# A spectral filter beside a two-layer network: fewer warm-up matmuls, remainder rows copied by ScalarE, and a new written-out order

## The chip, the cores and the metric

The kernel runs on one core of one Trainium2 chip. A core has five engines that work side by side, each with its own queue of instructions: TensorE (PE in the profile; its weight loads are shown as PEld), VectorE (DVE), ScalarE (ACT), GpSimd (POOL) and SyncE (SP), which here issues most DMAs. They share the on-chip memory SBUF (128 partitions); matmuls write to PSUM, eight banks of 512 fp32 values in each partition. The metric is the device time of one execution in microseconds (us), and what is compared is the median of several executions.

## The reference: what is computed

The input `x` has 2048 rows (tokens) of 640 values. It is normalised row by row, `xn = layernorm(x)`, and two branches that read `xn` are added to `x`:

```python
def _A_ref(x, w_r, w_i):                      # spectral filter
    X = rfft2(x, axes=(-2, -1))               # 2048 x 321 complex
    y = irfft2(X * (w_r + 1j * w_i), s=(2048, 640))
def _B_ref(x, w1, b1, w2, b2):                # two-layer network
    h = gelu(x @ w1 + b1)                     # 640 -> 1536
    return h @ w2 + b2                        # 1536 -> 640
return x + _A_ref(xn, ...) + _B_ref(xn, ...)
```

Inputs and output are bf16.

## The kernel before, in words

**Tiles.** The tokens are split into 16 tiles, c = 0 to 15, of 128 tokens each. Token 16p+c lies in partition p of tile c, so a tile is strided over the sequence, and the transform over the sequence splits into a step of length 128 and one of length 16.

**Norm.** For each tile DVE computes statistics (`stats`, L480, two halves; `mv`, L482), then `ve` (L490), POOL a power for `rstd` (L491), and DVE the normalised tile (L510). Norms are written to a buffer of two slots, each for a pair of tiles (`xn{pair}`, a part of the tensor `T`), so a pair's norm waits until all that read the slot's former pair is through.

**Network branch.** Layer 1 needs `xn` transposed (`xnT`). Tiles 0 to 3 are transposed by PE (L528, through `ident`) and copied from PSUM by DVE or ACT (L533 to L537). Tiles 4 to 15 are transposed by DMA, issued on SP (L519). Layer 1 of tiles 0 and 1 is cut into small pieces, so that each piece needs one slice of W1 (`hpsa`, L567 to L595); tiles 2 and 3, 4 to 7, 8 to 11 and 12 to 15 follow as blocks (`hps0` to `hps3`, L596 to L613). ACT applies the gelu and adds `b1col`. That column is made from the loaded row b1 by twelve tiny matmuls (L464, "b1 turned") and one copy on ACT (L466). Layer 2 accumulates twelve pieces per tile in PSUM (`second`, L758). For some tiles (`KEEP`) DVE moves its result to SBUF early (`kept`, L771).

**Spectral branch.** DVE folds each pair of normalised tiles twice (L540, L544), PE transforms along the tokens (`aps`, L550), then along the width (`bps`, table `etab`), then the length-16 step (`cps`). DVE multiplies with the filter `W` (L678, L682), PE goes back (`dps`), and DMA transposes on SP (L703) bring the result to `XV`. The last way back, `eps` (L726, table `getab`), works on six groups of chunks with 2, 3, 3, 3, 3, 2 chunks (`GROUPS`). Its weights are the columns of `XV` for chunk c: 128 values 16 elements apart. The width 160 of each quarter is split into 128 rows and 32 remainder rows; `width` (L615) makes for each chunk four 128-row matmuls and four 32-row ones, the remainders of the four quarters side by side in plane 4 of `XV`. DVE unfolds, a last matmul (L777) adds the result to layer 2 in PSUM, DVE writes the sum to `W1` (L780), and a DMA stores it.

**Start.** PE first multiplies zeros (`idle`, L409), in two ops of 39 and 8 matmuls, both ahead of the first transposes in the order.

**What sets the order.** Each piece of work is an "op" with a list of what it reads and writes. `ORDER` (L253) is a text that names each op once by its number, with the letter of its engine (s SP, p PE, a ACT, d DVE, g POOL) and its PSUM or buffer slots. `arrange` (L145) puts the ops into the five queues in that order, and `sync` (L161) derives the semaphore waits. Priorities, durations, landing times (`at=`), `gate` and `hard` fed the planner that once wrote the text; they have no effect on the program when `ORDER` is given. A queue works strictly in its order, so an op that waits holds all behind it on its engine.

Of the kernel before, what the change touches and what calls it, by code (L numbers as in the profile page):

```python
# [254 lines left out]
53a 289p:2 269p:1 23s 239p:5 259p:3 240p 127d 250p 24s 280p 270p 290p 133d:0 260p 25s 128p:4 130p:7 281p 129d 26s 251p 131a 132d 291p 261p 242p 252p 27s 241p 272p 68d 292p 271p 28s  # L255
243p 282p 69d 283p 253p 29s 262p 65d 244p 273p 274p 30s 284p 66d 254p 255p 70d 263p 67d 293p 245p 71d 134d:1 264p 72g 285p 135d 275p 137d 276p 256p 141d:0 278a 294p 246p 286p 144d
258a 142p:4 136d 248a 145p:7 143d 265p 247a 295p 146d 287a 266p 296p 148d:0 257a 305p:5 77d 288a 311p:7 147d 268a 323p:4 306p 85d 267a 314p:6 307a 312p 89d 315p 277a 332p:5 93d
297a 324p 92d 320p:3 298a 302p:0 101d 313a 321p 325a 100d 333p 326p:7 322a 152d:0 94d 308p:4 90d 316a 327p 151d 138p:1 91d 328a 139p 97d 309p 334a 95d 317p:6 98d 96g 140a 329p:7
102d 99d 330p 103d 149d 299p:5 5g 104g 184d:0 318p 331a 303p 150d 300p 182d 319a 7g 154p:1 81d 304a 153p 183s 197d:1 573p:6 301a 195d 310a 574p 186d:0 155a 196s 590p:4 187d 84d
575p 74d 591p 76d 198s 82d 576p 73d 592p 191d:1 185s 78d 189d 577p 188d 190d 578p 75d 83d 200d:0 31s 593p 79d 199d 32s 80g 192p:1 86d 594p 579d 33s 193p 113d 595p 34s 87d 203d:1  # L260
88g 374p:6 35s 204d 156d:1 375p 596d 157s 386p:0 376a 116d 377p:4 158d 194a 201d 159s 404p:7 114d 171d:0 398p:5 202d 115d 169d 36s 405p 161d:0 206p:1 172s 108d 406a 205p 117d 387p
207a 109d 389p:7 160d 170s 401p:6 118d 164d:1 388a 119d 165d 378p 120g 106d 37s 402p 163d 110d 379a 162d 390p 38s 221d:1 403a 399p 105d 39s 166p:0 223d 400a 167p 107d 356p:4 224s
111d 225d:0 391a 112g 226d 357p 359p:7 227d:1 358a 40s 229d 347p:5 228d 168a 230d 222s 173d:0 348p 174d 360p 210d:0 41s 231p:0 177d:0 361a 335p:6 208d 42s 349a 178d 232p 175d 336p
211s 176d 234a 212d:0 344p:7 213d 337a 180p:3 215d:1 209s 179p 216d 233a 345p 214d 350p:6 217d 181d 346a 43s 218p:0 219p 44s 365p:7 220a 45s 351p 338p:4 46s 352a 446p:0,0 47s 48s
366p 448d 447a 49s 339p 428p:5 50s 51s 443p:0,1 429p 445a 444d 410p:6 340a 733d 411p 367a 461p:0 434p:4 462a:1 463d:0 435p 430a 464p:0 436a 416p:5 235g 465d 466a 417p 412a 236g
471d:0 449p:0,1 418a 472d 237g 425p:7 450a 468d:1 238g 422p:4 467d 451a 426p 423p 469d:0 353p:5 473d:1 424a 470d 485p:0 427a 431p:4 487d:1 486a:0 432p 474d 626p:6 433a 478p:0
380p:4 480d:0 479a:2 381p 475p:0 382a 354p 477d 476a 419p:4 355a 484s 420p 488p:0 413p:5 490a 489d 483s 414p 421a 495d:1 455p:0,0 415a 481s 496d 392p:4 457a 456d 482s 383p:5 492d:0
393p 384p 394a 491d 452p:0,1 385a 498d:0 494d:1 368p:4 453a 454d 369p 341p:5 370a 497d 493d 512p:0 371p:4 513a:1 514d:0 372p 499p:0 373a 342p 500d:2 501a:0 362p:4 343a 363p 509p:0
395p:5 511d 510a 396p 515d:1 502p:0 627p 503a 504d 628p 364a 520d:0 505s 458p:0,1 397a 519d 629p 459a 507s 460d 609p:4 610p 516d 506s 536p:0 521d:0 630p 538a:0 518d:1 611p 517d
508s 537a:1 522d 631p 533p:0 612p 535a 534d 613p 632d 526p:0 614p 543d:0 527a:1 662p:6 540d:1 528a:2 663p 544d 523p:0 664p 615d 524a 665p 546d:1 525a 530s 645p:4 539d 666p 545d  # L270
667p 529s 541d:0 542d 646p 668d 647p 531s 547p:0 698p:6 548d:0 532s 699p 549d:1 700p 648p 550p:0 701p 551a 552d 702p 554s 703p 649p 704d 650p 556s 440p:7 651d 441p 553s 437p:4 442a
407p:5 555s 408p 564p:6 565p 438p 566p 557p:0 567p 558d:1 559a 568p 439a 560d:0 569p 409a 561d 583p:0 562d:0 563d 681p:4 585a:0 584d 570p 682p 571d:7 619p:0 586d:0 572g 587d 683p
620a:1 589d:1 684p 621a 588d 685p 686p 655p:0 687d 622d:0 600p:6 657a:0 743d 601p 623d 656a 602p 636p:4 580p:0 616p:2 581d:6 637p 638p 617d:2 639p 625d:0 618g 603p 624d 640p 658d:0
652p:2 604p 653d:0 641p 654g 605p 606p 642p 607d:3 691p:0 643d:5 608g 672p:6 659d 693a:1 644g 673p 692a 633p:4 674p 660d:0 675p 634d:7 676p 661d 635g 726p:0 695d:0 708p:4 582g
727a:0 694d 677p 728a 709p 678p 597p:0 679d:2 669p:2 710p 598d:0 680g 711p 688p:6 670d:7 712p 599g 697d:1 713p 696d 734p:0 689d:4 717p:2 714p 718p 690g 715d:5 719p 729d:0 671g 735p
730d 753p:7 720p 716g 705p:4 736p 706d:2 737p 732d:0 707g 721p 731d 722p 723p 738p 724d:1 739p 725g 744p:4 745p 746p 740p 747p 741d:7 754p 755p 748p 756p 749p 742s 750p 757p 762p:6
751d:0 758p 759p 763p 764p 760d 752s 765p 766p 767p 761s 768p 769d 770s
"""


# [9 lines left out]
AHEAD = 2  # L290
CHAIN = "b0 b1 c00 c01 b2 c10 c11 d00 d01 b3 b4 c20 c21 d10 d11 b5 c30 c31 d20 d21 d30 d31".split()
XASPLIT = [((0, 1, 2, 3, 4),)] * 7 + [((0, 1), (2, 3, 4))]
WARM = (39, 8)
FILTER = {7: 4}


def bass_parallel_sum__spectral_gfnet__dense_activation_gelu__prompt_kernel(
# [21 lines left out]
    with ExitStack() as es:  # L319
# [113 lines left out]
        for j, at in enumerate((5.92, 6.93, 7.9, 9.75, 10.7)):  # L433
            if j == 3:
                load_x(2, 2, next(pr), at=8.75)
            load(W1[:, F * j:F * j + F], w1v[:, j, :], B_w1s[j], 393216, prio=next(pr), at=at)
        load(gtab[:], const["G"], B_g, 524288, prio=next(pr), at=12.0)
        for c, at in zip(range(4, 16, 2), (13.2, 14.7, 15.5, 16.3, 17.1, 17.9)):
# [13 lines left out]
        for ri, wsrc in enumerate((A_w_r, A_w_i)):  # L452
            for half in range(4):
# [4 lines left out]
                else:  # L458
# [36 lines left out]
        for pair in range(8):  # L495
# [10 lines left out]
            for n in range(2):  # L506
# [15 lines left out]
                for j0, j1, engs in ((0, 2, ["dve"]), (2, 5, ["act"])) if c < 2 else ((0, 5, ["dve", "act"]),):  # L522
                    nj = j1 - j0
                    tps = Buf(f"tps{c}", psum, 1, ZONE["tps"])

                    def xt(e, _, n=n, xnv=xnv, tps=tps, j0=j0, j1=j1):
                        for j in range(j0, j1):
                            ins = e.transpose(psb(tps.slot, [[1, 512]]).bitcast(BF)[:, 128 * j:128 * j + 128], xnv(n, 128 * j, [[1, 128]]), ident[:])  # L528
                        return ins
                    tp = K.op([("pe", nj * mm_us(128))], pr, xt, reads=[B_xn, xn, B_id], writes=[tps], segs=[("128", nj * mm_us(128))])  # L530
# [290 lines left out]
```

## Time and profile before

| | us |
|---|---|
| median of 3 runs | 148.84 |
| lowest, highest | 148.66, 149.22 |
| the profiled execution | 149.58 |
| its span, first to last instruction | 147.8 |

| engine | busy us | share of the span |
|---|---|---|
| PE | 141.9 | 96% |
| PEld (weight loads) | 90.5 | 61% |
| DVE | 110.0 | 74% |
| ACT | 72.3 | 49% |
| POOL | 21.5 | 15% |

A row of the timeline reads: start, duration (of a run of like instructions together), engine, line, operation, output<-input, shape, count, and in brackets how long the engine was idle before it and what ended that. A row of the groups reads: busy time, mean ns of one, idle time before and its releasers. Durations of matmuls include their run through the array, so neighbours overlap: what a matmul costs the stream is the step from its start to the next start. PEclk, the granted clock, is 1.00 throughout, also where matmuls step slowly at the start. Some matmul records are missing from the trace (1677 of 1692).

### The profile page before, as it was taken

How to read it: one execution, taken by the hardware profiler on the slowest of the kernel's cores; microseconds unless marked ns; L12 is line 12 of the kernel's file. 1: busy time of each engine (PE TensorE's matmuls, PEld its weight loads, DVE VectorE, ACT ScalarE, POOL GpSimd, SP SyncE). 2: the span in 40 equal slices, each digit the busy share in tenths (PEclk: the TensorE clock that was granted, in tenths of full speed). 3: DMA queues.
4: the chain of work that ended last, by engine and by line, in shares of the span. 5: the costliest groups of instructions: out<-in, count | busy, mean ns of one | idle time of the engine just before them, and what ended most of it. 6: DMA issues, size and time to landing. Idle time of an engine off the chain costs nothing.

```text
span 147.8 us, 3951 instructions
## 1 busy us (share of the span) xinstructions
PE 141.9 (96%) x1677; PEld 90.5 (61%) x1692; DVE 110.0 (74%) x240; ACT 72.3 (49%) x118; POOL 21.5 (15%) x35
## 2 busy tenths in 40 slices
PE   7999999999799999999999999999999999999993
PEld 7999995655456645445644545555666656655573
DVE  2688999999996367856966979864099787769543
ACT  3615995047598579977775756121075400430000
POOL 1002040301200005000000000000002024545620
DMA  5999999569999998988700670475302107777974
GB/s 119 305 402 399 378 388 132 113 141 135 165 163 160 158 161 218 350 334 45 141 4 0 41 138 10 89 93 106 71 4 24 20 4 84 93 89 91 114 87 114
DMA packets 29843, 21.01 MB, mean 142 GB/s; under 512 B 20225, under 2 KB 27137, under 8 KB 29826
## 3 DMA queue, kind: packets, MB, share of 16 engines
q1 hardware_dynamic: 27232, 15.84, 49.7%
q0 software_dynamic: 2592, 4.92, 17.8%
q8 instruction: 13, 0.21, 0.6%
q14 instruction: 4, 0.03, 0.1%
q10 hardware_dynamic: 2, 0.00, 0.0%
HBM read 13.54 MB, written 5.24 MB: 127 GB/s over the span
## 4 chain that ended last, share of the span: by engine, by line
PE 89%; DVE 5%; DMA 2%; issue 2%; SPq 1%
PE ps L383 88%; DMA xnT<-T 2%; DVE W L780 1%; DVE stats L480 1%; PE ps L528 1%; DVE T L544 1%; DVE T L510 1%; DVE T L540 1%; DVE X L771 1%; SPq L519 1%; DVE mv L482 0%; DVE warm L399 0%; DVE ve L490 0%
## 5 line engine op out<-in xcount | busy, mean ns | idle before, releaser
L383 PE MATMUL ps<-xnT,W 128*128 128x512 bf16 (+2 forms) x336 | 56.9, 320 | 1.0 <-DMA xnT<-T 1.0
L383 PE MATMUL ps<-W,gT 128*128 128x128 bf16 (+3 forms) x382 | 55.0, 292 | 1.5 <-issue 1.0
L383 PEld LDWEIGHTS ps<-W,gT 128*128 128x128 bf16 x396 | 30.1, 98 | 22.5 <-issue 1.7
L383 PEld LDWEIGHTS ps<-xnT,W 128*128 128x128 bf16 x336 | 31.4, 114 | 18.5 <-ACT gT L611 2.8
L611 ACT ACTIVATE gT<-ps,b1col 128x512 bf16<-128x512 f32 (+1 forms) x48 | 28.4, 638 | 15.1 <-PE ps L383 15.1
L787 POOL DMA_DIRECT2D out_dram<-W x14 | 12.3, 990 | 71.0 <-DVE W L780 71.0
L394 ACT ACTIVATE Wf<-ps 128x960 bf16<-128x960 f32 (+1 forms) x10 | 8.5, 888 | 17.9 <-PE ps L383 17.9
L480 DVE BATCH_NORM_STATS2 stats<-X 128x6 f32<-128x320 bf16 x32 | 14.0, 477 | 2.1 <-DMA X<-in_A_x_dram 2.1
L678 DVE TENSOR_TENSOR T<-Y,Wf 128x1288 bf16<-128x1288 bf16 x16 | 12.5, 822 | 0.0
L491 POOL TENSOR_TENSOR rstd<-ve,mhalf 128x2 f32<-128x2 f32 (+1 forms) x8 | 6.0, 744 | 31.9 <-DVE ve L490 31.8
L395 DVE CAST Y<-ps 128x644 bf16<-128x644 f32 x7 | 5.8, 829 | 5.4 <-PE ps L383 5.4
L394 ACT ACTIVATE Xb<-ps 128x960 bf16<-128x960 f32 (+1 forms) x7 | 8.0, 1166 | 3.4 <-PE ps L383 3.3
L544 DVE TENSOR_TENSOR T<-T 128x512 bf16<-128x512 bf16 (+1 forms) x32 | 9.0, 313 | 0.2
L394 ACT ACTIVATE XV<-ps 128x1280 bf16<-128x1280 f32 (+2 forms) x8 | 8.9, 1109 | 0.5 <-PE ps L383 0.5
L395 DVE CAST Xb<-ps 128x960 bf16<-128x960 f32 (+1 forms) x5 | 5.5, 1105 | 4.2 <-PE ps L383 4.2
L394 ACT ACTIVATE Y<-ps 128x644 bf16<-128x644 f32 x9 | 6.3, 708 | 4.1 <-PE ps L383 4.0
L510 DVE TENSOR_SCALAR T<-X,mv,rstd 128x640 bf16<-128x640 bf16 x16 | 6.9, 441 | 1.5 <-POOL rstd L491 1.0
L383 PE MATMUL ps<-getab,XV 32*128 32x160 bf16 (+1 forms) x128 | 7.5, 242 | 0.0
L540 DVE TENSOR_TENSOR T<-T 128x640 bf16<-128x640 bf16 x16 | 7.4, 480 | 0.1
L739 DVE TENSOR_TENSOR Wf<-Wf 128x960 bf16<-128x960 bf16 (+1 forms) x12 | 6.7, 596 | 0.9 <-PE ps L383 0.8
L780 DVE TENSOR_TENSOR W<-ps,b2bc 128x640 bf16<-128x640 f32 x6 | 4.8, 821 | 3.3 <-PE ps L383 3.3
L383 PE MATMUL ps<-etab,XV 32*128 32x160 bf16 (+1 forms) x128 | 7.2, 232 | 0.0
(53 smaller groups left out, 123.1 us busy)
## 6 DMA issues: line engine op xcount, KB each, us to landing
out_dram<-in_A_x_dram POOLq DMA_DIRECT2D x4, 640.0 KB, 7.3
X<-in_A_x_dram SPq DMA_DIRECT2D x7, 320.0 KB, 9.4
out_dram<-W POOLq DMA_DIRECT2D x14, 160.0 KB, 3.4
W<-in_B_w_dram SPq DMA_DIRECT2D x5, 384.0 KB, 5.8
W<-in_B_w_dram SPq DMA_DIRECT2D x3, 640.0 KB, 12.8
Wf<-in_A_w_r_dram SPq DMA_DIRECT2D x7, 160.5 KB, 3.9
Wf<-in_A_w_i_dram SPq DMA_DIRECT2D x7, 160.5 KB, 4.6
gtab<-c_G SPq DMA_DIRECT2D x1, 512.0 KB, 9.1
```

What stands on the lines that cost most here:

```text
L383: ins = e.matmul(o_, lhsT=lw, rhs=rh, start=st, stop=sp_, skip_group_check=True)
L394: return e.activation(dst(), src(), ACT.Copy, scale=scale)
L395: return e.tensor_copy(dst(), src())
L480: st_ops.append(K.op([("dve", 0.393)], pr, lambda e, _, c=c, h=h: e.bn_stats(stats[:, c, 6 * h:6 * h + 6], view(X, c * D + H2 * h, [[1, H2 ...
L510: o = K.op([("dve", 0.356)], pr, lambda e, _, c=c, n=n, xnv=xnv: e.tensor_scalar(out=xnv(n, 0, [[1, D]]), in0=view(X, c * D, [[1, D]]), sc ...
L540: K.op([("dve", 0.39)], pr, lambda e, _, k=k, op=op, xnv=xnv, x1v=x1v: e.tensor_tensor(out=x1v(H2 * k, [[D, 2], [1, H2]]), in0=xnv(0, 0, [ ...
L544: ring_ops.append(K.op([("dve", 0.333 if w == 128 else 0.136)], pr, lambda e, _, op=op, x1v=x1v, xfv=xfv, o_=o_, o0=o0, o1=o1, w=w: e.tens ...
L611: K.op([("act", act_us(128 * nt, 1) + 0.02)], pr + PRIO["gelu"], lambda e, _, c0=c0, nt=nt, fc=fc, hps=hps: e.activation(gT[:, fc, 128 * c ...
L678: filt_ops.append(K.op([("dve", 0.738)], pr, lambda e, _, k=k, Y=Y, TB=TB, pair=pair: e.tensor_tensor(out=view(TT, TB.slot * 8 * KP + k * ...
L739: K.op([("dve", 0.068 + n / 6)], pr + 3, lambda e, _, k=k, op=op, y2=y2, yf=yf, n=n: e.tensor_tensor(out=view(Wf, YF + yf.slot * 3 * D + ( ...
L780: K.op([("dve", dve_us(w))], 95, lambda e, _, os_=os_, fps=fps, o0=o0, w=w, xo=xo, base=base: e.tensor_tensor(out=view(W1, OST + os_.slot ...
L787: last.append(K.op([("pool", 0.9)], 450, lambda e, _, c=c, os_=os_: e.dma_start(ov[:, c, :], view(W1, OST + os_.slot * D, [[1, D]]), accum ...
```

## The change

- The warm-ups are one op of 31 matmuls instead of two of 39 and 8; the matmuls that turn b1 come right behind them, ahead of the first transposes (before: behind these).
- For the last four groups of the way back (gi 2 to 5) ACT first copies the remainder plane's columns of the group to `T`, chunk by chunk side by side, and the 32-row matmuls take their weights from that copy. The 128-row ones and the first two groups stay as they are. PE waits for the copy (`B_xr`).
- `ORDER` is written anew. Among much else: on SP the loads of `etab` and `mtab` move behind the DMA transposes of tiles 8 to 11; all five of the first W loads (before: four) come ahead of the transposes of tiles 4 to 7, whose order is now 5, 6, 7, 4 (before: 4, 5, a W load, 7, 6). On DVE the copy for tile 1 moves ahead of the two foldings of tile 0, tile 2's copy goes to ACT, and the norm of tile 8 loses some work ahead of it. A few PSUM copies swap between ACT and DVE. Behind the filter, more of layer 2 stands between the last DMA transposes and the first group of the way back.
- The changed `at=` values, durations and `hard=` only concern the planner.

```diff
-9s 2a 0d 4g 6g 125p:1 3g 11a 10s 8p:6 12s 13s 14s 15s 55d 54d 16s 1d 17s 56d 60d 57a 18s 58a 59d 121d:1 19s 61d 124p:1 20s 122p:0 52p:7 62d 21s 123d 126a 63d 64g 22s 279p:0 249p:6
...
+9s 2a 0d 7g 8p:1 3g 11a 10s 5g 4g 12s 13s 14s 15s 54d 55d 16s 1d 17s 56d 60d 57a 52p:3 18s 58a 59d 121d:1 19s 61d 122p:0 20s 124p:2 62d 21s 53a 63d 123d 125a 64g 22s 238p:5 288p:4
...
-WARM = (39, 8)
+WARM = 31
...
-        idle(WARM[0], 0.1067 * 32 + (WARM[0] - 32) * mm_us(128))
+        idle(WARM, WARM * mm_us(128))
...
-        pe([("128", 0.7)], 200, lambda: [(psb(B_b1ps.slot, [[1, 1]], fc), part(gT, 0, 1, 512 * (fc // 4) + fc % 4, [[4, 128]]), ident[0:1, 0:1], True, True)
+        b1op = pe([("128", 0.5)], 200, lambda: [(psb(B_b1ps.slot, [[1, 1]], fc), part(gT, 0, 1, 512 * (fc // 4) + fc % 4, [[4, 128]]), ident[0:1, 0:1], True, True)
...
-                    if j0 and not c:
-                        idle(WARM[1], WARM[1] * mm_us(128), gate=[tp])
...
-            pe(five_segs(n, 0.045), pr, lambda c0=c0, n=n, eps_=eps_: five(
-                eps_.slot, n, lambda i, g, p0, k: part(XV, p0, k, 2048 * g + c0 + i, [[16, 128]]), getab),
-                reads=B_v + [B_ge], writes=[eps_], gate=[fin_ops[c0 - 5]] if c0 > 8 else [])
+            B_xr = Buf(f"xr{gi}")
+            if gi > 1:
+                K.op([("act", act_us(128 * n) + 0.18 * n)], pr + 5, lambda e, _, c0=c0, n=n: e.activation(
+                    view(TT, 128 * c0, [[128, n], [1, 128]]), view(XV, 4 * 2048 + c0, [[1, n], [16, 128]]), ACT.Copy), reads=B_v, writes=[B_xr], after=filt_ops)
+            pe(five_segs(n, 0 if gi > 1 else 0.052 * (n - 1)), pr, lambda c0=c0, n=n, eps_=eps_, gi=gi: five(
+                eps_.slot, n, lambda i, g, p0, k: part(TT, p0, k, 128 * (c0 + i), [[1, 128]]) if gi > 1 and g == 4 else part(XV, p0, k, 2048 * g + c0 + i, [[16, 128]]), getab),
+                reads=B_v + [B_ge, B_xr], writes=[eps_], gate=[fin_ops[c0 - 5]] if c0 > 8 else [])
```

The numbers of ops shift by one between the two texts behind op 124, and by up to four near the end.

More of the change, by code (lines that the diff above doesn't have):

```diff
@@ new lines @@
+278p:7 268p:3 23s 248p:2 258p:1 126d 249p 24s 279p 239p 289p 127p:0 25s 259p 129p:6 128d 269p 26s 260p 132d:0 130a 280p 241p 281p 131d 251p 27s 291p 292p 282p 66d 261p 28s 283p
+242p 293p 68d 271p 272p 290p 69d 270p 262p 263p 284p 65d 240p 273p 70d 252p 67d 294p 134d:0 264p 71d 135d 72g 285p 136d 250p 295p 133d 286a 253p 254p 297a 140d:1 274p 255p 296a
+143d 265p 141p:0 256a 146d:0 144p:4 142a 243p 244p 145d 245p 287a 275p 147d 310p:0 267a 74d 301p:4 246a 77d 325p:6 247a 326p 148d:1 331p:7 257a 151d 76d 332p 327a 302p 92d 311p
@@ new lines @@
+34s 193a 157d:1 385p:6 35s 155d 595d 397p:7 36s 386p 170d:0 158s 201d 373p:5 168d 387a 202d 398p 109d 169s 376p:6 108d 399a 105d 374p 203d 116d 377p 171s 375a 106d 403p:4 159d:0
+404p 114d 156s 205p:1 118d 160d 405a 204p 115d 400p:7 119d 206a 110d 164d:0 120g 161d 388p:5 37s 107d 162d 163d 401p 38s 378a 111d 112g 389p 222d:1 39s 165p:0 220d 390a 166p 40s
+343p:6 224d:0 402a 225d 223s 344p 167a 229d:1 355p:7 228d 227d 226d 334p:4 221s 345a 173d:0 356p 172d 231p:0 209d:0 357a 230p 41s 177d:0 358p:5 175d 207d 232a 42s 176d 335p 233a
@@ L278 @@
+715p 716p 747p:6 717d:7 748p 724p 718g 737p:0 758p 707p:4 725p 738p 726d:6 739p 708d:0 727g 749p 740p 733d 741p 709g 734d:0 742p 735d 750p 746d 743p 751p 744d:2 765p:4 752p 759p
+753p 760p 745s 761p 754d:7 766p 767p 762p 768p 755s 769p 763d 770p 771p 764s 772d 773s
 """
@@ L432, in bass_parallel_sum__spectral_gfnet__dense_activation_gelu__prompt_kernel @@
         load(part(gT, 0, 1, 0, [[1, F]]), b1v, B_b1t, 3072, q="act", prio=409, at=3.2)
-        for j, at in enumerate((5.92, 6.93, 7.9, 9.75, 10.7)):
+        for j, at in enumerate((6.05, 7.05, 8.0, 9.85, 10.8)):
             if j == 3:
-                load_x(2, 2, next(pr), at=8.75)
+                load_x(2, 2, next(pr), at=8.85)
             load(W1[:, F * j:F * j + F], w1v[:, j, :], B_w1s[j], 393216, prio=next(pr), at=at)
-        load(gtab[:], const["G"], B_g, 524288, prio=next(pr), at=12.0)
-        for c, at in zip(range(4, 16, 2), (13.2, 14.7, 15.5, 16.3, 17.1, 17.9)):
+        load(gtab[:], const["G"], B_g, 524288, prio=next(pr), at=12.3)
+        for c, at in zip(range(4, 16, 2), (13.7, 14.9, 15.7, 16.55, 17.35, 18.15)):
             load_x(c, 2, next(pr), at=at)
@@ L529, in xt @@
                         return ins
-                    tp = K.op([("pe", nj * mm_us(128))], pr, xt, reads=[B_xn, xn, B_id], writes=[tps], segs=[("128", nj * mm_us(128))])
-                    if j0 and not c:
-                        idle(WARM[1], WARM[1] * mm_us(128), gate=[tp])
+                    tp = K.op([("pe", nj * mm_us(128))], pr, xt, reads=[B_xn, xn, B_id], writes=[tps], hard=[b1op], segs=[("128", nj * mm_us(128))])
                     us = {"dve": 0.06 + 0.068 * nj, "act": act_us(128 * nj)}
```

38 lines of the change are left out of this document (15 added, 23 removed).

## The prediction

> **What bounds the kernel now.** I read the page first, then the chain that ended last, then the waits and the timelines of single engines. "Spacing" is the step from one start to the next.
>
> ```profile
> span 147.8 us, 3951 instructions
> ...
> PE 89%; DVE 5%; DMA 2%; issue 2%; SPq 1%
> ```
>
> TensorE (PE) carries nine tenths of the chain, so what leaves its stream leaves the time, but only if no wait behind takes it back. One real wait is left in the middle of the stream:
>
> ```profile
> 37.52 0.72 PE L383 MATMUL ps<-gtab,T 128*128 128x128 bf16 x10
> 39.21 2.10 PE L383 MATMUL ps<-xnT,W 128*128 128x512 bf16 x9 [0.97 <-DMA xnT<-T]
> ```
>
> At 39.21 the first layer-1 work of tiles 4 to 7 starts. It needs all four DMA transposes of these tiles, and came 0.97 us too early for the last. So PE's start can improve by any amount without moving 39.21; the SyncE (SP) queue that issues the transposes must. SP's timeline:
>
> ```profile
> 10.89 0.63 SPq L375 DMA_DIRECT2D etab<-c_E  x1
> 11.57 0.69 SPq L375 DMA_DIRECT2D mtab<-c_M  x1
> 21.77 6.16 SPq L519 DMA_TRANSPOSE xnT<-T  x4
> 27.98 0.58 SPq L375 DMA_DIRECT2D ntab<-c_N  x1
> 28.60 2.68 SPq L375 DMA_DIRECT2D Wf<-in_A_w_r_dram  x4
> 31.33 2.61 SPq L519 DMA_TRANSPOSE xnT<-T  x2
> 33.98 0.59 SPq L375 DMA_DIRECT2D Wf<-in_A_w_r_dram  x1
> 34.62 3.15 SPq L519 DMA_TRANSPOSE xnT<-T  x2
> ```
>
> From 21.77 to 37.77 the queue never rests: 16.0 us of issue, released by the norm of tile 8. A pair of transposes takes 2.61, so 1.3 each; by that the first four (6.16) hold 0.95 too much and the last pair (3.15) 0.55. I call these the two long issues; the page does not say what made them.
>
> **The change, part by part.** *The start.* Warm-ups, transposes, turned b1 and first matmuls on PE, then VectorE (DVE), then the loads:
>
> ```profile
> 0.99 5.19 PE L383 MATMUL ps<-warm 128*128 128x128 bf16 x47 [0.99 <-DVE warm L399]
> 5.98 0.74 PE L528 MATMUL ps<-ident,T 128*128 128x128 bf16 x5
> 6.65 0.55 PE L383 MATMUL ps<-ident,gT 1*128 1x1 bf16 x12
> 7.13 1.53 PE L383 MATMUL ps<-xnT,W 128*128 128x128 bf16 x24
> ```
>
> ```profile
> 4.72 0.45 DVE L510 TENSOR_SCALAR T<-X,mv,rstd 128x640 bf16<-128x640 bf16 x1
> 5.08 0.49 DVE L480 BATCH_NORM_STATS2 stats<-X 128x6 f32<-128x320 bf16 x1
> 5.60 0.21 DVE L482 BATCH_NORM_AGGREGATE mv<-stats 128x2 f32<-128x12 f32 x1
> 6.75 0.29 DVE L395 COPY xnT<-ps 128x256 bf16<-128x256 bf16 x1 [0.94 <-PE ps L528]
> 6.96 0.14 DVE L490 TENSOR_SCALAR ve<-mv 128x1 f32<-128x1 f32 x1
> 7.79 0.45 DVE L510 TENSOR_SCALAR T<-X,mv,rstd 128x640 bf16<-128x640 bf16 x1 [0.69 <-POOL rstd L491]
> ...
> 12.46 0.80 DVE L510 TENSOR_SCALAR T<-X,mv,rstd 128x640 bf16<-128x640 bf16 x2 [0.33 <-POOL rstd L491]
> 13.18 0.42 DVE L544 TENSOR_TENSOR T<-T 128x512 bf16<-128x512 bf16 x1
> 13.69 0.89 DVE L395 COPY xnT<-ps 128x640 bf16<-128x640 bf16 x2
> ```
>
> ```profile
> 1.66 1.38 SPq L375 DMA_DIRECT2D W<-in_B_w_dram  x3
> 3.08 0.43 SPq L375 DMA_DIRECT2D X<-in_A_x_dram  x1
> ```
>
> and, from the view of DMA issues, the first of each of these two (last column: us to landing):
>
> ```profile
> W<-in_B_w_dram SPq DMA_DIRECT2D x1, 384.0 KB, 4.8
> X<-in_A_x_dram SPq DMA_DIRECT2D x1, 320.0 KB, 6.2
> ```
>
> A warm-up costs (5.98-0.99)/47 = 106 ns. 31 end at 4.3, the twelve b1 matmuls (6.65 to 7.13, 0.5) at 4.75; then PE idles until tile 0's norm ends (4.72+0.45 = 5.17). Its five transposes run from 5.2 to 5.8, DVE's copy ends near 6.2, and the first real matmul waits for the first slice of W1 (issued 1.66, landed 4.8 later: 6.5). That is 0.6 ahead of 7.13. By itself I count it at nothing: the wait at 39.21 covers it, unless that wait goes.
>
> *The clock, put at risk by the same edit.* The 24 matmuls at 7.13 run at about 1.53/24 = 64 ns or less, the 47 and the five transposes at 106. So the pace doubled between 6.4 and 7.1, 5.4 to 6.1 us after the first matmul, with PE issuing all along; after 3.8 us it was still slow. In the changed kernel PE stops at 4.75, after 3.8 us, and stutters until 6.5. Bounds for the faster pace: no later than before (6.7), or 5.7 after the restart at 6.5 (12.2). I take 9.5, the middle, since nothing here shows how a gap counts.
>
> [...]
>
> *What a late clock costs DVE.* In the new order DVE's copy for tile 1 stands ahead of the foldings of tile 0 and waits for a transpose behind twenty layer-1 matmuls; PE then does the rest of tiles 0 and 1 before it transposes tiles 2 and 3, whose copy (13.69) DVE must make. At the fast pace the first copy ends near 8.5, DVE folds tile 0 in two steps of about 0.45 (the size of the one at 13.18) and goes on at 9.4, no earlier than X for tiles 2 and 3 lands (3.08+6.2 = 9.3): as before. With the slow pace until 9.5, PE loses 3.0 x (1-60/106) = 1.3 (60 for the fast step), of which some 0.3 would else have been waits for the next slices of W1. So the first copy and then the transposes and copies of tiles 2 and 3 come late, the latter by 1.0 (bounds: 0, and 2.2 with the turn at 12.2); I take 1.0. PE's own loss lies inside its 0.6 lead, the wait of 0.97 and the later landing.
>
> *DVE's list up to the norm of tile 8.* It loses the tile-2 copy, now on ScalarE (ACT; 0.89/2 = 0.45), a folding (0.42) that moves from 13.18 into the wait before 12.46, a norm (0.45) and a statistics step (0.49), and gains two statistics steps (0.98): 0.8 earlier, if the clock is as before.
>
> *SP's queue.* The loads of `etab` and `mtab` (10.89 and 11.57; 0.68 and 0.68 with the gaps) move behind the first four transposes: 1.37 more in the stretch of 16.0. The fifth W load moves ahead of the four transposes of tiles 4 to 7, which all stand ahead of the last one's end in either order: 0. So the last issue moves by -0.8 + 1.37 = +0.57 with a fast clock, +1.57 with the late one. The two long issues may vanish (-1.5) or stay (0); half, -0.75, since neither end is shown. Result: -0.2 (fast), +0.8 (late). Everything behind 39.21 on PE moves by that. `etab` and `mtab` are read only in the steps behind layer 1 of tiles 4 to 7; no cost. On POOL one more memset stands ahead of the identity matrix, which is first read at 4.3, and on ACT b1's copy goes ahead of a copy whose input comes later: 0.
>
> *The four new ACT copies.* The remainder matmuls of the way back (`getab`) and of the way in (`etab`), by form, and ACT's timeline at the way back:
>
> ```profile
> L383 PE MATMUL ps<-getab,XV 32*128 32x160 bf16 x64 | 2.5, 250 | 0.0
> ...
> L383 PE MATMUL ps<-etab,XV 32*128 32x160 bf16 x64 | 2.2, 231 | 0.0
> ```
>
> ```profile
> 107.64 1.26 ACT L611 ACTIVATE gT<-ps,b1col 128x512 bf16<-128x512 f32 x2
> 109.98 0.97 ACT L394 ACTIVATE Wf<-ps 128x960 bf16<-128x960 f32 x1 [1.08 <-PE ps L383]
> ```
>
> The remainder weights `getab` reads come 16 elements apart, those of `etab` side by side: 2.5 against 2.2 us for six groups, 0.05 a group. Four groups become contiguous: -0.2 (bounds 0 and -0.3). Each copy has 384 elements or fewer; bounds by ACT rows 0.3 (a third of 0.97) and 0.97. ACT idles 1.08 before 109.98 and more later, so they hide; without that cover the first would hold the group evacuations up to 1 us.
>
> *A new wait on DVE.* Tile 4's transpose becomes the last of the four, and the norms of tiles 14 and 15 overwrite its source:
>
> ```profile
> 37.14 0.45 DVE L510 TENSOR_SCALAR T<-X,mv,rstd 128x640 bf16<-128x640 bf16 x1 [0.44 <-DMA xnT<-T]
> ...
> 44.19 1.03 DVE L544 TENSOR_TENSOR T<-T 128x128 bf16<-128x128 bf16 x4
> 46.37 0.72 PE L383 MATMUL ps<-gtab,T 128*128 128x128 bf16 x10
> ```
>
> Now the norm starts with the landing that also releases PE. Behind it are the foldings that took until 45.2, 8.1 us, of which 0.7 now run ahead: 7.4. PE comes to the matmuls that need the last of them 46.37-39.21 = 7.2 after its own start: a new wait of about 0.2 (bounds 0 and 1.0, since DVE's rest is in the same file). The remaining reorder carries the same work; I cost it at 0, within 0.3 either way, as PE there waits for nothing worth a row.
>
> **Sum.** Late clock: +0.8 - 0.2 + 0.2 = +0.8; with both long issues kept +1.6. The profiled execution took 149.58, of which 147.8 is span; the median of the runs is 148.84, 0.74 lower. I carry the difference over: 148.84+0.8 is 149.6.
>
> **The rivals.**
> - *The clock rises as before.* For it: the first 3.8 us are unbroken. Against it: in this trace 3.8 us had not been enough. -0.2-0.2+0.2 gives 148.6: no change.
> - *Faster: SP's queue runs free.* Clock as before and both long issues gone: 0.57-1.5-0.2+0.2 = -0.9, 147.9. For it: ten of twelve transposes took 1.3. It decides if the wait at 39.21 ends before 38.5. Against it: nothing in the edit touches what made them long.
> - *DVE's wait lies on the path in full.* If the foldings behind the late norm reach PE 1.0 late, on either clock, 149.6 to 150.7.
> - *The copies don't do what they say.* Strided reading elsewhere in the group hides the gain: 0 instead of -0.2, no change of sign.
>
> **How the numbers follow.** Late clock 0.5 (slower by over 0.5% in 0.35 of it, within in 0.15); clock as before 0.25 (within 0.2, slower 0.05); SP free 0.15 (faster); DVE's wait in full 0.1 (slower). 0.5%, 0.74 us, is about what this kernel's measurement tells from no change. So faster 0.15, same 0.35, slower 0.5. Range: from near the SP rival, 148.1, to the late clock with long issues kept and some of DVE's wait, 150.8. The forecast's own range is 149.0 to 150.8.
>
> **What would show it.** PE's first layer-1 matmuls at 6.5, and their mean step 106 ns past 7 (late clock) or about 60. SP's first transposes start at 21.0 (fast) or 22.0 (late). The wait before the first 128x512 of tiles 4 to 7 grows to 1 to 2 us and ends at 39.0 to 40.8. DVE's first norm behind it waits 2 us or more for a transpose. The `getab` remainder group falls to 2.3. It is wrong if that wait ends before 38.5, or if PE shows new waits over 0.5 behind 50 us.

## The result, and the profile after

| us | before | after |
|---|---|---|
| median | 148.75 (4 executions, 148.64 to 149.22) | 150.88 (4 executions, 150.55 to 151.16) |
| the profiled execution | 149.58 | 150.95 |
| its span | 147.8 | 149.2 |

The changed kernel is slower: ratio 1.0136, 95% interval 1.0106 to 1.0167. The forecast was 149.6 with a range up to 150.8, which the median passes by 0.1. The sign was right. The cause given for it was not, as the trace shows first. Ratios, here and below, leave out disturbed executions (over 1.5% above the fastest of the same kernel), the medians do not.

The page of the changed kernel, its span and its chain that ended last:

```profile
span 149.2 us, 3943 instructions
...
PE 71%; DVE 19%; issue 4%; DMA 2%; SPq 2%; POOL 0%; DVEq 0%
```

PE carried 89% of the chain before. Now the chain leaves PE and goes through DVE and SP, which points at a transfer that released PE late. PE's timeline, at the start and in the middle:

```profile
0.99 3.49 PE L383 MATMUL ps<-warm 128*128 128x128 bf16 x31 [0.99 <-DVE warm L399]
4.41 0.55 PE L383 MATMUL ps<-ident,gT 1*128 1x1 bf16 x12
5.29 0.45 PE L528 MATMUL ps<-ident,T 128*128 128x128 bf16 x5 [0.32 <-DVE T L510]
6.32 1.49 PE L383 MATMUL ps<-xnT,W 128*128 128x128 bf16 x20 [0.58 <-DVE xnT L395]
...
36.95 0.72 PE L383 MATMUL ps<-gtab,T 128*128 128x128 bf16 x10
40.07 2.97 PE L383 MATMUL ps<-xnT,W 128*128 128x512 bf16 x13 [2.39 <-ACT XV L394]
42.91 0.73 PE L383 MATMUL ps<-gtab,T 128*128 128x128 bf16 x10
43.48 3.40 PE L383 MATMUL ps<-xnT,W 128*128 128x512 bf16 x15
46.72 0.72 PE L383 MATMUL ps<-gtab,T 128*128 128x128 bf16 x10
47.62 0.73 PE L383 MATMUL ps<-gtab,T 128*128 128x128 bf16 x10 [0.17 <-DVE T L542]
```

*The start* came as forecast: the first layer-1 matmuls at 6.32, 0.8 earlier than before. *The clock* did not: the five transposes took 0.45 us where they took 0.74 before, so in this execution the faster pace was there by 5.3, earlier than before the change (an early or a late clock, here and below, means when this pace comes: the granted clock reads 1.00 from 0 to 12 us in both traces, at the slow pace too). *The wait* is 2.39 us instead of 0.97 and ends at 40.07 instead of 39.21. The releaser that the row names (ACT, through at 39.55) is not the real one: in the trace with the tables back, below, PE starts this same work at 37.34, before ACT comes to that instruction (38.14). SP's timeline and DVE's show what was missing:

```profile
20.52 5.77 SPq L519 DMA_TRANSPOSE xnT<-T  x4
26.34 0.58 SPq L375 DMA_DIRECT2D etab<-c_E  x1
26.96 0.43 SPq L375 DMA_DIRECT2D mtab<-c_M  x1
27.43 0.44 SPq L375 DMA_DIRECT2D ntab<-c_N  x1
27.91 3.32 SPq L375 DMA_DIRECT2D Wf<-in_A_w_r_dram  x5
31.28 5.26 SPq L519 DMA_TRANSPOSE xnT<-T  x4
```

```profile
36.02 0.16 DVE L490 TENSOR_SCALAR ve<-mv 128x2 f32<-128x2 f32 x1
40.06 0.80 DVE L510 TENSOR_SCALAR T<-X,mv,rstd 128x640 bf16<-128x640 bf16 x2 [3.88 <-issue]
...
46.53 1.03 DVE L542 TENSOR_TENSOR T<-T 128x512 bf16<-128x512 bf16 x4
```

SP was through with the last of the four transposes (tile 4) at 36.54 (31.28+5.26), against 37.77 before: the queue had become 1.2 us faster. Yet DVE's norm of tiles 14 and 15, which may start only when that transpose has landed, and PE started together at 40.06. The last transpose landed 0.9 us later (39.98 against 39.12) after an issue 1.2 us earlier. The views of DMA issues for the moment of the last issue, of after and of before (last column: us from issue to landing):

```profile
xnT<-T SPq DMA_TRANSPOSE x1, 4.7
```

```profile
xnT<-T SPq DMA_TRANSPOSE x1, 2.6
```

What lay between is in the page's list of DMA queues (packets, MB, share of the engines' time), in a row that stands in both pages alike, and in the same list for the stretch from 37.2 to 38.6 of the changed kernel:

```profile
q8 instruction: 13, 0.21, 0.6%
```

```profile
q8 instruction: 1, 0.02, 6.2%
```

Thirteen packets of 16 KB on an "instruction" queue are counted on the same 16 DMA engines. PE has 1676 recorded matmuls and 1676 recorded weight loads, 3352 in all, 258 for each packet; that the packets fetch PE's instructions is the author's reading, from this count and from how they move with PE's instructions in the experiments. One of them runs from 37.36 for 1.4 us (6.2% of 16 engines over the stretch of 1.4 us), right on the transpose in flight. Before, the matching one ran from 34.28, for 1.1. The experiments test this.

*The copies.* PE's groups by form:

```profile
L383 PE MATMUL ps<-etab,XV 32*128 32x160 bf16 x64 | 2.2, 231 | 0.0
...
L383 PE MATMUL ps<-getab,T 32*128 32x160 bf16 x44 | 1.5, 231 | 0.0
L383 PE MATMUL ps<-getab,XV 32*128 32x160 bf16 x20 | 0.8, 252 | 0.0
```

The 44 matmuls of the copied groups take 231 ns, as the contiguous ones with `etab` do; the 20 of the first two groups still take 252.

*A pause that no wait names.* The third place is a small step of the spectral branch, from the timelines of PE, after and then before:

```profile
67.52 0.85 PE L383 MATMUL ps<-Xb,mtab 32*32 32x322 bf16 x32
```

```profile
67.25 0.49 PE L383 MATMUL ps<-Xb,mtab 32*32 32x322 bf16 x32
```

The 32 matmuls are one operation, with its waits ahead of the first. After the 28th PE stands still for 0.35.

**Where the 1.37 us between the two profiled executions went**, by the starts of the same work in both traces: +0.86 at 40.07 (landing); +0.33 ahead of 47.62 (PE waits for the foldings behind DVE's late norm, of which the last four start at 46.53: ten such matmuls take 0.57 to the next start, 42.91 to 43.48, but 0.90 from 46.72 to 47.62; the 0.17 of the row is less, since the modelled end of the matmul before runs into the gap); +0.35 (the pause); -0.2 (copies): 1.34. The medians lie 2.13 apart, since the profiled execution of the kernel before (149.58) is slower than all four that its median is of; for these 0.8 us more there is no trace.

### The profile page after: what moved, and what is told of

The parts are those of the page before. It is cut to its first block, busy times and chain, and to the rows that moved or that the text cites. A ratio compares the mean times of both kernels' runs of the same rounds, so it can differ in the third digit from the quotient of the medians.

```text
span 149.2 us, 3943 instructions
## 1 busy us (share of the span) xinstructions
PE 142.3 (95%) x1676; PEld 88.6 (59%) x1676; DVE 109.1 (73%) x237; ACT 76.4 (51%) x125; POOL 21.5 (14%) x35
## 4 chain that ended last, share of the span: by engine, by line
PE 71%; DVE 19%; issue 4%; DMA 2%; SPq 2%; POOL 0%; DVEq 0%
PE ps L383 71%; DVE stats L480 7%; DVE T L542 4%; DVE T L510 3%; DVE T L538 3%; SPq L519 2%; DMA X<-in_A_x_dram 2%; DVE mv L482 1%; DMA xnT<-T 1%; PE ps L528 1%; DVE xnT L395 0%; POOL rstd L491 0%; DVE ve L490 0%; DVE X L773 0%; DVE W L782 0%
## 5 line engine op out<-in xcount | busy, mean ns | idle before, releaser
L383 PE MATMUL ps<-xnT,W 128*128 128x512 bf16 (+2 forms) x336 | 57.9, 320 | 3.0 <-ACT XV L394 2.4
L383 PE MATMUL ps<-W,gT 128*128 128x128 bf16 (+3 forms) x396 | 57.4, 295 | 0.0
L609 ACT ACTIVATE gT<-ps,b1col 128x512 bf16<-128x512 f32 (+1 forms) x48 | 29.3, 637 | 11.1 <-PE ps L383 10.9
L394 ACT ACTIVATE Wf<-ps 128x960 bf16<-128x960 f32 (+1 forms) x9 | 7.6, 880 | 13.0 <-PE ps L383 13.0
L394 ACT ACTIVATE Y<-ps 128x644 bf16<-128x644 f32 x10 | 6.9, 707 | 4.9 <-PE ps L383 4.9
L542 DVE TENSOR_TENSOR T<-T 128x128 bf16<-128x128 bf16 (+1 forms) x32 | 8.8, 312 | 0.2
L395 DVE CAST Y<-ps 128x644 bf16<-128x644 f32 x6 | 5.0, 827 | 4.0 <-PE ps L383 4.0
L773 DVE TENSOR_TENSOR X<-ps,b2bc 128x640 f32<-128x640 f32 x7 | 5.8, 823 | 2.4 <-PE ps L383 2.4
L680 DVE TENSOR_TENSOR Z<-T 128x644 bf16<-128x644 bf16 x16 | 7.0, 486 | 0.1
```

Source lines behind the costliest of these rows:

```text
L383: ins = e.matmul(o_, lhsT=lw, rhs=rh, start=st, stop=sp_, skip_group_check=True)
L394: return e.activation(dst(), src(), ACT.Copy, scale=scale)
L395: return e.tensor_copy(dst(), src())
L542: ring_ops.append(K.op([("dve", 0.333 if w == 128 else 0.136)], pr, lambda e, _, op=op, x1v=x1v, xfv=xfv, o_=o_, o0=o0, o1=o1, w=w: e.tens ...
L609: K.op([("act", act_us(128 * nt, 1) + 0.02)], pr + PRIO["gelu"], lambda e, _, c0=c0, nt=nt, fc=fc, hps=hps: e.activation(gT[:, fc, 128 * c ...
L680: K.op([("dve", 0.402)], pr, lambda e, _, TB=TB, Z=Z, r=r, op=op: e.tensor_tensor(out=view(Zb, Z.slot * 4 * KP + r * KP, [[2 * KP, 2], [1, ...
```

## The experiments

Three explanations of the late landing stood against each other. That a fetch of PE instructions delays the transposes in flight, and sixteen fewer warm-ups (32 PE instructions) push it from 34.3 to 37.4, onto the last one (theory F). That PE's earlier start does it by itself (theory S). That the new order on SP does it. The late clock stayed as a fourth. The first four expectations were written ahead of these names and call their theories A to C. The kernel before itself measured medians of 148.75 to 149.35 beside the different experiments, so versions are compared by their ratios to it. In the short diffs, a word such as 156s is an op in the order's text; 156s to 171s are the transposes of tiles 4 to 7, 182s is the first of tiles 8 to 11, 29s and 30s load `etab` and `mtab`.

**Tile 4 first** (changed kernel)

```diff
-... 158s ... 169s ... 171s ... 156s
+... 156s ... 158s ... 169s ... 171s
```

> The changed kernel with one edit: SP issues the four transposes of tiles 4 to 7 in the order 4, 5, 6, 7 (changed kernel: 5, 6, 7, 4). Theory A, it matters which tile is last because DVE's norm of tiles 14 and 15 waits for tile 4: DVE's wait of 3.9 us falls below 1, the 0.3 us that PE then waits for the folding is gone, and the time falls by 0.3 to 1.2 us against the changed kernel (150.9). Theory B, it matters when the last of the four lands, whichever tile it is: the layer-1 work of tiles 4 to 7 still starts near 40.0, and only the 0.3 us is won. Theory C, the start or the order behind 50 us costs the time: no difference.

150.75 (4 executions), ratio 1.011 (1.005 to 1.017). DVE's wait fell from 3.88 to 0.36, so the order did make it. The time hardly moved: in this trace the clock rose late (the first layer-1 matmuls, 20 of them, took 2.32 us, 106 ns each), and the last transpose was issued at 37.01. It landed 2.45 later; the fetch came at 44.1. PE's wait ended at 39.55, only 0.34 behind the kernel before. The larger part of this trace's loss is the pause inside the small step, 0.95 here (from the start of the 28th matmul to that of the 29th) against 0.35:

```profile
66.65 0.48 PE L384 MATMUL ps<-Xb,mtab 32*32 32x322 bf16 x28
67.79 0.32 PE L384 MATMUL ps<-Xb,mtab 32*32 32x322 bf16 x4 [0.65 <-issue]
```

0.34, 0.95 and the copies' -0.2 make 1.09 of the 1.14 by which the span is longer than before (148.93 against 147.79).

**Tables back** (changed kernel)

```diff
-182s ... 184s ... 195s ... 197s ... 29s ... 30s
+29s 30s 182s ... 184s ... 195s ... 197s
```

> The changed kernel with one edit: the loads of etab and mtab are issued on SP ahead of the transposes of tiles 8 to 11, as before the change. Theory B (SP's queue up to the last of the four transposes sets the time): the last transpose is issued 1.1 us earlier (34.2 instead of 35.3) and the wait of PE ends 1.0 to 3.3 us earlier (36.7 to 39.0 instead of 40.07; the lower end if the landing then takes 2.6 us as before the change, not 4.7); the time is 148.2 to 150.0. Rival, the landing waits for something that does not move with the issue: the wait still ends near 40 and the time stays at 150.9.

149.71 (10 executions, 148.45 to 150.48), ratio 1.0026 (0.9989 to 1.0062): undoing this one part takes back most of the loss. PE's timeline:

```profile
6.38 1.31 PE L384 MATMUL ps<-xnT,W 128*128 128x128 bf16 x20 [0.58 <-DVE xnT L396]
...
37.34 2.97 PE L384 MATMUL ps<-xnT,W 128*128 128x512 bf16 x13
...
64.62 0.48 PE L384 MATMUL ps<-Xb,mtab 32*32 32x322 bf16 x28
65.76 0.32 PE L384 MATMUL ps<-Xb,mtab 32*32 32x322 bf16 x4 [0.65 <-issue]
```

No wait at 37.34 any more. The last transpose was issued only 0.64 earlier than in the changed kernel (34.62), but landed at 37.07, 2.45 later, just ahead of the fetch at 37.11. This profiled execution, with an early clock, took 148.66. The pause inside the small step is 0.95 here too.

**47 warm-ups** (changed kernel)

```diff
-WARM = 31
+WARM = 47
```

> The changed kernel with one edit: 47 warm-ups instead of 31, still ahead of the turned b1. Theory B: the start lies behind the wait before tiles 4 to 7, so first real matmuls at about 7 instead of 6.3 change the time by less than 0.3 us, unless the clock rises late. It also puts 32 more instructions into PE's stream, so fetches of instructions that fall at other moments show in how long the last transpose takes to land. Theory C (the shorter warm-up costs time): 1 us or more faster than the changed kernel.

150.03 (10 executions), ratio 1.0049 (1.0023 to 1.0075). The wait fell to 0.87 and ended at 38.59: the fetch stood at 34.66 again, the last transpose was issued at 35.12 as before it, and landed at 38.50, 3.38 later instead of 4.72. The gain on the changed kernel, 0.9% by the ratios, is more than the 0.3 us that theory B of the expectation allowed; the trace puts it down to the landing.

**The start alone** (kernel before)

```diff
-WARM = (39, 8)
+WARM = (23, 8)
-... 124p ... 122p ... 52p
+... 52p ... 124p ... 122p
```

> The kernel before with the start edit alone: 31 warm-ups and the turned b1 ahead of the first transposes, all else in the order of before. Theory B: the wait before tiles 4 to 7 grows by what the start wins (0.5 to 0.9 us) and ends where it ended, 39.2; the time is 148.4 to 149.0. If the clock rises late in it: first matmuls step at 106 ns, and up to 1 us slower. Theory C (the start costs the time): slower by 1 us or more with the clock up early.

150.59 (6 executions), ratio 1.0068 (1.0028 to 1.0109). Sixteen fewer warm-ups and the early b1 are enough to lose 0.7%, on the old order of SP:

```profile
37.39 0.72 PE L384 MATMUL ps<-gtab,T 128*128 128x128 bf16 x10
40.03 2.32 PE L384 MATMUL ps<-xnT,W 128*128 128x512 bf16 x10 [1.93 <-DMA xnT<-T]
```

The wait doubled, from 0.97 to 1.93. The loss is that of theory C and not the 148.4 to 149.0 of theory B, and it speaks against the new order on SP as the cause. Fetch at 37.23, last issue 35.95, landing 39.94.

**The same warm-up time with fewer instructions** (kernel before). This tells F from S: 16 of the warm-ups are twice as wide and replace 32, so the warm-up keeps its length, but the fetch moves.

```diff
-[(psb(b.slot, [[1, 128]]), warm[:], warm[:], True, True) for _ in range(n)]
+[(psb(b.slot, [[1, 256]]), warm[:], view(warm, 0, [[0, 2], [1, 128]]), True, True) for _ in range(wide)]
+  + [(psb(b.slot, [[1, 128]]), warm[:], warm[:], True, True) for _ in range(n - 2 * wide)]
```

> The kernel before with one edit: the same 5.0 us of warm-up in 31 matmuls instead of 47 (16 of them 256 columns wide), so 32 instructions fewer in PE's stream and nothing else moved. Theory F (a 16 KB fetch of PE's instructions goes through the same DMA engines, and while it runs the transposes do not land): the fetch that lay at 34.3 falls at 37 to 38, the last transpose of tiles 4 to 7 is issued at 35.9 to 36.5 and lands 3.5 to 4.7 us later, and the wait of PE ends at 39.6 to 40.6 instead of 39.2; 0.4 to 1.4 us slower than the kernel before. Theory S (the earlier start or the order costs it, not the number of instructions): the same time as the kernel before, within 0.3.

150.33 (9 executions), ratio 1.0075 (1.0038 to 1.0113): the same loss as with the start alone, without any of the start's edits.

```profile
0.99 5.00 PE L383 MATMUL ps<-warm 128*128 128x128 bf16 x31 [0.99 <-DVE warm L399]
...
6.69 1.53 PE L383 MATMUL ps<-xnT,W 128*128 128x128 bf16 x24
...
37.25 0.72 PE L383 MATMUL ps<-gtab,T 128*128 128x128 bf16 x10
39.82 3.40 PE L383 MATMUL ps<-xnT,W 128*128 128x512 bf16 x15 [1.84 <-issue]
```

Fetch at 37.39, last issue 35.16, landing 39.73: 1.3 earlier issued and 0.6 later landed than before. PE's real work starts 0.4 ahead of before, half of the other runs' lead, but an earlier PE can't make a landing later while its issue comes earlier: theory S falls.

**Padding behind b1** (changed kernel, and the same with the tables back): 16 one-column matmuls of no use add 32 instructions without 16 warm-ups' time.

```diff
+ + [(psb(B_b1ps.slot, [[1, 1]], 100 + k), part(gT, 0, 1, 0, [[4, 128]]), ident[0:1, 0:1], True, True) for k in range(16)]
```

> The changed kernel with one edit: 16 one-column matmuls behind the turned b1, so that PE's stream has as many instructions as before the change. Theory F: the fetch falls near 34.7 as with 47 warm-ups, the last transpose lands 2.5 to 3.4 us after its issue, the wait of PE ends at 38 to 39 instead of 40.07, and the time is 0.5 to 1.8 us lower than the changed kernel where the clock rises early. Theory S: no difference.

> Both: etab and mtab ahead of the transposes as before the change, and the 16 one-column matmuls. Theory F: the wait ends at 37.3 to 38.3, and the time is 148.3 to 149.5; not better than with the tables alone, where the fetch came after the last landing.

150.80 (4 executions), ratio 1.0119 (1.0063 to 1.0175), and 149.88 (10 executions), ratio 1.0058 (1.0025 to 1.0092). The first is a miss: the clock rose late in its trace, SP issued the transposes 1.5 us later, and the fetch, at 36.82, met the last one all the same (landing 3.62 later, wait ended at 40.43). It decides nothing on F. In the second the clock rose, fell back at 7.1 and rose again at 10.5; the work of tiles 4 to 7 starts at 38.94 without a wait. That start and the median both lie above what was expected.

**A cold start** (tables back, every warm-up one column wide, `[[1, 1]]` instead of `[[1, 128]]`): what a late clock costs where no wait covers it.

> The changed kernel with etab and mtab back, and its 31 warm-ups cut to one column each: as many instructions, but PE's array rests until the first transposes at 5.3. The clock must then rise late, 9 us or later. Theory L (a late clock holds DVE's list and with it SP's first transposes): first matmuls step at 106 ns, SP's first transposes start at 21.4 to 22.7 instead of 20.35, and the time is 1.0 to 2.4 us above that of the early executions with the tables back (148.5). Rival (the slow stretch is covered by waits): less than 0.5 above.

150.59 (10 executions), ratio 1.0111 (1.008 to 1.0142). Timeline of PE:

```profile
5.30 0.71 PE L529 MATMUL ps<-ident,T 128*128 128x128 bf16 x5 [2.12 <-DVE T L511]
6.33 2.32 PE L384 MATMUL ps<-xnT,W 128*128 128x128 bf16 x20 [0.32 <-DVE xnT L396]
...
38.53 2.97 PE L384 MATMUL ps<-xnT,W 128*128 128x512 bf16 x13
```

38.53 against 37.34 with the tables back and an early clock: 1.2 us at that place, 1.0 in the span (147.9 against 146.9), as the expectation's theory L has it.

**Longer warm-ups with the tables back**: 47 matmuls, or 31 of which 16 are twice as wide.

> The changed kernel with the two table loads back ahead of the transposes of tiles 8 to 11 on SP, and 47 warm-ups instead of 31. If the clock's late rise in part of the executions is what held the version with the tables back at 149.7 (theory: 31 warm-ups are too few to be safe), its executions now lie closer together, the first layer-1 matmul starts near 6.6 with steps of about 60 ns behind 7, and the median is 148.7 to 149.2: 32 more PE instructions put PE's third instruction fetch back to about 34.6, among the issues of the last four transposes, which then land near 38, 0.3 to 0.7 behind PE. If the clock has no part in it: 149.7 again, or a wait that ends near 38.5 as with 47 warm-ups alone and 150.0.

> The same with 31 warm-ups of which 16 are twice as wide: the time of 47 warm-ups with the instruction count of 31. Both theories together (clock safe by 5 us of warm-up; third instruction fetch of PE stays near 37.1, behind the landing of the last transpose): no wait before the first 128x512 of tiles 4 to 7, that work starts near 37.5, span 146.9 to 147.2, median 148.4 to 148.8, and at or under the kernel before. If the late rise is a matter of chance that the length of the warm-up does not touch: 149.7 and executions from 148.4 to 150.5, as with the tables back alone. If the fetch does not matter: the same as its neighbour with 47 narrow ones.

149.56 and 149.57 (12 executions each), ratios 1.0028 (1.0006 to 1.0051) and 1.0029 (1.0006 to 1.0053). The executions lie closer (148.8 to 149.8 and 148.75 to 149.95), as the expectation has it if a late clock spread them, but neither reached its forecast. In both traces the first layer-1 matmul starts at 7.2 to 7.3, not 6.6, and where no wait covers it that costs its full 0.8 to 0.9: the second, whose fetch came at 40.0 as wanted, starts tiles 4 to 7 at 38.25 without a wait, 0.91 behind 37.34. It then loses more: DVE waits for a load of the filter, and PE for DVE. The rows of the two timelines, DVE first:

```profile
57.88 3.05 DVE L678 TENSOR_TENSOR T<-Y,Wf 128x1288 bf16<-128x1288 bf16 x4 [1.81 <-DMA Wf<-in_A_w_i_dram]
```

```profile
63.39 0.52 PE L384 MATMUL ps<-Z,ntab 32*32 32x320 bf16 x32 [1.31 <-issue]
```

What a short warm-up gains when the clock rises early (0.9 here), it gives back when it rises late (1.2 in the cold start).

**Strided weights again** (tables back; the copies are made and waited for, but not read)

```diff
-part(TT, p0, k, 128 * (c0 + i), [[1, 128]]) if gi > 1 and g == 4 else part(XV, ...)
+part(TT, p0, k, 128 * (c0 + i), [[1, 128]]) if False else part(XV, ...)
```

> The changed kernel with the tables back, where the 32-row matmuls of the last four groups read the remainder plane of XV again, 16 elements apart, while ACT still makes its copies and PE still waits for them. If the strided weights are what the copies save: the getab remainder matmuls go back from 159 to about 208 ns mean span for groups of three and from 89 to 139 for the group of two, 0.05 us a group, 0.2 in all; one time between 148.7 and 150.5, which cannot show it. If the saving came from elsewhere, the groups keep 159 and 89.

150.77 in one execution, with a late clock. The groups by form and the pause:

```profile
L384 PE MATMUL ps<-getab,XV 32*128 32x160 bf16 x64 | 2.5, 250 | 0.0
```

```profile
66.25 0.49 PE L384 MATMUL ps<-Xb,mtab 32*32 32x322 bf16 x28
67.67 0.32 PE L384 MATMUL ps<-Xb,mtab 32*32 32x322 bf16 x4 [0.93 <-issue]
```

64 matmuls at 250 ns, as before the change. The starts of the third to the sixth group of the way back lie 1.90, 1.95, 2.02 and 2.06 behind those of the trace with the tables back: 0.05 a group, which is what the copies save.

**Eight wide warm-ups** (tables back; 8 matmuls of 512 columns in place of 31 of 128)

```diff
-[(psb(b.slot, [[1, 128]]), warm[:], warm[:], True, True) for _ in range(n)]
+[(psb(b.slot, [[1, 512]]), warm[:], view(warm, 0, [[0, 4], [1, 128]]), True, True) for _ in range(8)]
```

> The changed kernel with the tables back, and the warm-up of 31 matmuls made in 8 of four times the width: 3.4 us as before, but 46 PE instructions fewer ahead of everything. With the tables back, PE paused 0.95 us (1.22 with the strided groups) inside the second small step of the first filter pair, after the 28th of 32 like matmuls of one operation, which hence wait for no data. In every trace of the new order that pause, 0.27 to 1.22 us long, lies behind the same count of recorded PE instructions (1442 to 1444), also where 16 warm-ups more move it to another matmul, and the long ones end 1.2 to 1.4 us after an instruction fetch ends. If it is PE running out of instructions at a block's end, the end now falls among 128x512 matmuls behind that step, where a fetch has time: no pause inside a small step above 0.15, and the time falls by 0.5 to 1 against the version with the tables back: median 148.7 to 149.2, an execution with the early clock 147.6 to 148.0 (span 146.0). If the pause belongs to that operation (its data, its PSUM bank), it stays where it is, 0.9 long, and the median is 149.6 to 149.8. Third fetch behind 40: no wait before the first 128x512 of tiles 4 to 7.

149.34 (12 executions, 147.89 to 150.78), ratio 0.9997 (0.9965 to 1.0029); the median forecast was 148.7 to 149.2. The pause is gone:

```profile
67.16 0.50 PE L384 MATMUL ps<-Xb,mtab 32*32 32x322 bf16 x32
```

So it belonged to a place in PE's instruction stream and not to the operation. (The expectation's "in every trace of the new order" is too wide by one: the run with 16 wide ones, where PE had waited 1.31 us shortly before, has no pause.) The shortest execution of all kernels, 147.89, is here, but in the profiled one the clock fell back for 3.4 us (mean 0.989), and the executions lie 2.9 us apart. Its median lies 0.3 above that of the kernel before (149.0). No version here beats the kernel before by what can be measured.

**All traces together.** The last of the four transposes of tiles 4 to 7 on SP and the start of PE's fetch nearest to it, from the traces' DMA records (us):

```
kernel                       issued  landed   lag   fetch
before                        36.48   39.12  2.64   34.28
same time, fewer instr.       35.16   39.73  4.56   37.39
start alone                   35.95   39.94  3.99   37.23
after                         35.26   39.98  4.72   37.36
tile 4 first                  37.01   39.46  2.45   44.08
tables back                   34.62   37.07  2.45   37.11
47 warm-ups                   35.12   38.50  3.38   34.66
padding                       36.72   40.34  3.62   36.82
tables back, padding          35.24   38.59  3.35   35.36
tables back, cold start       35.69   38.15  2.46   40.36
tables back, 47 warm-ups      35.31   38.86  3.55   35.34
tables back, 16 wide          35.13   37.59  2.46   40.01
tables back, strided          36.26   38.69  2.44   44.37
tables back, 8 wide           36.94   39.39  2.45   44.86
```

Where no fetch lies between issue and landing, the lag is 2.44 to 2.46 in six traces out of six. Where a fetch starts while the transpose is issued or in flight, or up to 0.5 us ahead, it is 3.35 to 4.72, in seven out of seven. (2.45 of "tables back" ends as its fetch begins; 2.64 of before follows a fetch that ended 1.1 ahead of the issue and had held up the transposes in front of it.) The count of instructions does not set a fetch's time alone. With the count of before (five traces) this one starts at 34.3 to 36.8. With 32 fewer it starts at 37.1 to 37.4 in four traces and at 40.0 to 44.4 in four others, three of which had a late clock (tile 4 first, cold start, strided). So in some executions of the changed kernel it may miss the last transpose, as it did with tile 4 first.

The issue on SP itself is longer too: 1.70 to 2.30 for the five transposes during or right behind a fetch, 1.27 to 1.30 for the rest of this block.

## Why the prediction was right or wrong

- *What bounds the kernel, and the start counted at nothing:* right in the changed kernel. The wait for the four transposes covered the 0.8 us. With the tables back and no wait, the same lead counts in full (38.25 against 37.34).
- *The late clock, the likeliest case:* failed for the profiled execution. The step that has PE stop at 4.75 and so puts the turn at 9.5 is the one: the pace rose by 5.3. The moment was right where a late clock occurs, and its price, taken as 1.0, was 1.4 to 2.0: in three other traces with 31 such warm-ups (tile 4 first, padding, strided) matmuls stepped at 106 ns up to 9.8, 10.3 and 10.4, and SP's first transposes began at 21.9 to 22.5 (forecast: turn at 9.5, transposes at 22.0; with the early clock 20.5, forecast 21.0). In two more (tables back with padding, 8 wide) the faster pace came early, was lost again at 7.1 and 8.6, and returned 3.4 us later in both; the mean granted clock is 0.988 over the span of 148.0 and 0.989 over 148.5, which makes about 0.5 in a stretch of 3.4 if all that is missing falls into it (an estimate), and matmuls step at 107 ns there and at 56 outside. Ahead of the first rise it reads 1.00 also where matmuls step at 106 (before, up to 6.4), so there the step tells and not the granted clock. Whether it rises early differs between executions, and the price in the changed kernel is small as far as one late trace tells (with the padding, 151.24 against 150.95), since the wait covers it.
- *SP's queue:* the last issue moved by -1.22, not by -0.2. DVE's list gave -1.25 (-0.8 forecast), the tables +1.09 (+1.37), and the long issues fell by 0.39 of 0.95 and by all of 0.55 (half forecast). The remaining -0.1 is not traced. "Nothing in the edit touches what made them long" was wrong: both had a PE fetch beside them (from 22.52 and 34.28), and the number of warm-ups helps to place the fetches (this second one starts at 37.23 with the start alone).
- *The landing,* taken as following the last issue as before: the step that decides. It took 4.72 instead of 2.64, +2.08, and turned a gain of 1.22 into a loss of 0.86. No case of the prediction had it. That the sum has the right sign, and that the wait ended between 39.0 and 40.8 as forecast, is luck: the wrong clock (+1.0) stands about where the landing should. The size was low, +0.8 against +1.37 between the profiled executions and +2.13 between the medians.
- *"SP's queue runs free"* came true as far as the issues go, and gave nothing.
- *The copies:* -0.2, as taken, by the strided run's starts; the 231 of the new form against 252 point the same way.
- *The new wait on DVE:* 3.9 us there and 0.33 on PE, against 0.2 with bounds 0 and 1.0. Right in kind, and the run with tile 4 first removes the wait on DVE. The rival's 149.6 to 150.7 leaves out the copies' -0.2; with it the same terms give 149.4 to 150.4.
- *The remaining reorder, 0 within 0.3:* the pause of 0.35, which no part had, and which is as large a term as the landing where it is longer (0.95 with tile 4 first, 1.22 in the strided run). Its cause is shown as far as that it keeps its place in PE's stream (behind 720 to 722 recorded matmuls in the nine traces that have it, also where 16 warm-ups move it to another matmul of the step) and goes away when 46 instructions fewer stand ahead. In six of the nine it ends 1.2 to 1.4 us after a fetch has ended. That PE runs out of instructions there is the author's reading; no record shows it.

Open: how one 16 KB packet holds up a transpose for 2 us, and why the clock rises early in one execution and late in the next. The ratios of after and of the tables back lie 1.1% apart, some 1.6 us, while a single trace each shows 2.3; of the other executions only a mean granted clock is on record, which does not tell when it rose or where the fetches lay.

## What to carry to other kernels

The number of instructions on an engine is a schedule of its own: here a 16 KB packet came for every 258 recorded PE instructions on average, on the same DMA engines as the data, and 32 instructions fewer moved one from 34.28 to 37.39 us (same time, fewer instructions), so an edit that adds or removes a few cheap instructions early can move one onto the transfer that a later stage waits for. Where a landing is later than its issue explains, compare the instruction queue of both traces before blaming the order. And a forecast that moves an issue by some tenths should bound its landing too: both 2.64 and 5.04 us stood among the transposes of the trace before.

## What was not expected of the hardware

- A 16 KB instruction packet of 1.0 to 1.4 us made a DMA transpose land 0.9 to 2.3 us late (2.45 to 3.35 and 4.72).
- PE stood still for 0.27 to 1.22 us inside one operation of 32 small matmuls, which takes 0.43 us to the next start without it (67.25 to 67.68 before), at a fixed place in the instruction stream.
- With the same 31 warm-up matmuls, the faster pace was there at 5.4 us in three traces, came at 9.8 to 10.4 in three others, and was lost again for 3.4 us in one.
